# Two more PSUM banks for the first batch's transposes and head pairs, and the second batch's keys loaded ahead of w_in

## The chip, the cores and the metric

One core of one Trainium2 chip (trn2). The metric is the device time of the whole kernel in microseconds; runs of one kernel mostly agree within 0.3%.

## The reference

Grouped attention followed by a feed-forward layer with squared ReLU, cut to what matters:

```python
q: (8, 16, 384, 64)   k, v: (8, 4, 384, 64)      # batch, heads, tokens, head size
attn = softmax(q @ k.T / 8) @ v                   # four query heads share one key head
x = attn as (3072, 1024)
out = max(x @ w_in, 0)**2 @ w_out                 # w_in (1024, 2048), w_out (2048, 1024)
```

## The kernel before

Work goes batch by batch. Scores of a batch go to PSUM banks 0 to 3, ACT takes their exponentials, "head pairs" multiply these with the values, their outputs are transposed to x, and the feed-forward tiles of one batch are interleaved with the scores of the next. Of the eight PSUM banks, 6 and 7 are meant for the feed-forward layer.

The order in which TensorE's instructions stand is not written by hand. A Python program (the recorder) keeps a clock for each engine and an estimated end for each load, made of constants in the code, and at each step places the candidate that its estimates call ready, by rank: score bursts 0, first batch's transposes 1, head pairs 2, transposes of outputs 3, second batch's transposes 4.5, feed-forward pieces 5. Second, the chip then runs TensorE's instructions in that fixed order: a semaphore wait (the engine standing still until another engine or a load reports that it is done) that the estimates thought over holds all that stands behind it.

```python
def pick(allowed):                       # which PSUM bank
    i = min(allowed, key=lambda i: (max(R.when(writes=[("bank", i)]), R.clock["tensor"]), used[i]))
...
# GpSimd's own order at the start: loads (with a cast to bf16) and copies
load_q(0, 8, 12, 0.6); load_q(0, 12, 16, 0.6)
dup_k(0, 1, 2)
load_w_in(0)
dup_k(0, 2, 3)
load_k(1)                                # second batch's keys
dup_k(0, 3, 4); aug_v(0, "gpsimd")
load_q(1, 0, 8); load_q(1, 8, 16)
load_w_in(1); load_v(1)
dup_k(1)                                 # one copy of 1.47 us
for i in range(2, 6): load_w_in(i)
aug_v(1, "gpsimd")
for i in range(6, 8): load_w_in(i)
...
LOW, MID, HIGH = tuple(range(6)), (4, 5), (6, 7)
...                                      # in the loop that places TensorE's work:
first = bool(sc_q) and sc_q[0][0] == 0   # scores of the first batch still to place
spare = MID if first else tuple(i for i in LOW if i not in held)
...
if turn_q and (b == 0 or pairs < 6 or x_done[0] == 8) and ...:
    cand.append((max(R.when(reads=src), open_bank(spare)) + wait, 3.5 * b + 1, "turn"))
...
ready = [x for x in cand if x[0] <= now + (0.0 if split else 0.05)]
what = min(ready, key=lambda x: x[1]) if ready else min(cand)
```

The softmax here doesn't subtract the row's maximum and nothing guards it: scores larger than these inputs give would overflow.

Of the kernel before, what the change touches and what calls it, by code (L numbers as in the profile page):

```python
# [141 lines left out]
def bass_gqa_attention__then__ffn_squared_relu_kernel(  # L142
# [64 lines left out]
    def load_k(b, after=()):  # L207
        st = b % NST
        R.add("gpsimd", lambda g: g.dma_start(  # L209
            k_st[st].ap().rearrange("p (g j) d -> p g (j d)", j=NJ),  # L210
            k[b].rearrange("g (p j) d -> p g (j d)", j=NJ)),
            reads=after, writes=[("k_st", st)], dma=f"k{st}", cost=1.1, issue=0.8)
# [19 lines left out]
    def load_v(b):  # L232
        st = b % NST
        R.add("gpsimd", lambda g: g.dma_start(
            v_st[st].ap().rearrange("p (g j) d -> p g (j d)", g=HKV),
            v[b].rearrange("g (p j) d -> p g (j d)", j=NJ)),
            writes=[("v_st", st)], dma=f"v{st}", cost=1.1, issue=0.8)

    def load_q(b, h0, h1, spread=0.0):
        st = b % NST  # L240
        i = R.add("gpsimd", lambda g: g.dma_start(  # L241
            q_st[st][:, h0:h1, :],
            q[b, h0:h1].rearrange("h (p j) d -> p h (j d)", j=NJ)),
            writes=[("q_st", st, h // 4, h % 4 // 2) for h in range(h0, h1, 2)], dma=f"q{st}_{h0}",
            cost=0.265 * (h1 - h0), issue=0.8)
        R.ops[i]["end"] += spread
# [4 lines left out]
    def load_w_in(i):  # L251
        R.add("gpsimd", lambda g: g.dma_start(
            w_in_sb[:, :, i * WC:(i + 1) * WC],
            moe_w_in[:, i * WC:(i + 1) * WC].rearrange("(c p) f -> p c f", p=128)),
            writes=[("w_in", i)], dma=f"wi{i}", cost=2.65, issue=0.9)
# [9 lines left out]
    def dup_k(b, g0=0, g1=HKV):  # L265
        n = (g1 - g0) * NJ
        src = (k_st[b % NST] if b else k_f32)[:, g0 * NJ:g1 * NJ, :].unsqueeze(2).to_broadcast([128, n, 2, D])
        dst = k_dup[b % 2][:, g0 * NJ:g1 * NJ, :, :]
        eng = "scalar" if b > 1 and not stretch[0] else "gpsimd"
        R.add(eng, lambda e: e.copy(dst, src) if eng == "scalar" else e.tensor_copy(dst, src),  # L270
              reads=[("k_st", b % NST) if b else ("k_f32", g) for g in range(g0, g1)],
              writes=[("k_dup", b % 2, g, x) for g in range(g0, g1) for x in range(2)], cost=0.125 * n)

    def aug_v(b, eng):
        R.add(eng, lambda e: e.tensor_copy(v_aug[b % 2][:, :, 0:D], v_st[b % NST][:, :, :]),  # L275
              reads=[("v_st", b % NST)], writes=[("v_aug", b % 2)], cost=0.4 if eng == "vector" else 0.85)
# [166 lines left out]
    held = set()  # L443
# [117 lines left out]
    load_q(0, 8, 12, 0.6)  # L561
    load_q(0, 12, 16, 0.6)
    dup_k(0, 1, 2)
    load_w_in(0)
    dup_k(0, 2, 3)
    load_k(1)
    dup_k(0, 3, 4)
    aug_v(0, "gpsimd")
    load_q(1, 0, 8)
    load_q(1, 8, 16)  # L570
    load_w_in(1)
    load_v(1)
    dup_k(1)
    for i in range(2, 6):
        load_w_in(i)
    aug_v(1, "gpsimd")
# [33 lines left out]
    LOW, MID, HIGH = tuple(range(6)), (4, 5), (6, 7)  # L610
# [63 lines left out]
    while av_q or av_open or sc_q or o_q or lanes or ff["now"] or ff["tiles"] or ff["down"]:  # L674
        now = R.clock["tensor"]
        first = bool(sc_q) and sc_q[0][0] == 0
        spare = MID if first else tuple(i for i in LOW if i not in held)
        if loaded + 1 < B and turned >= loaded and not turn_q:
            loaded += 1
            if loaded == 2:  # L680
# [163 lines left out]
```

## Time and profile before

| | before |
|---|---|
| median of 6 runs (lowest to highest) | 419.69 us (419.38 to 420.42) |
| span of the profiled run | 418.2 us |
| TensorE busy | 413.4 us, 99% |
| the first batch's twenty exponentials on ACT | 5.79 to 22.60 us, no pause |
| first row-split feed-forward tile (start of the interleaved part) | 28.75 us |
| wait for w_in block 3 there | 0.37 us |

Read it so: TensorE is busy for 99% of the span; in the first 23 us it follows ACT. The lines are in the prediction.

### The profile page before, as it was taken

Reading aid. Unit: us, or ns where it says so; the run is one execution under the profiler, and the core shown is the slowest. Engines: PE = TensorE matmul, PEld = TensorE weight load, DVE = VectorE, ACT = ScalarE, POOL = GpSimd, SP = SyncE. Lnnn points to the kernel's source line nnn. Section 1 sums busy time; section 2 is a strip of 40 time slices with the busy share of each in tenths; the row PEclk is TensorE's granted clock in tenths of the full one; section 3 lists DMA queues with packets and bytes.
Section 4 is the critical chain, followed back from the end, with each engine's and each line's share of the span. In section 5 each row is a group of like instructions: output and inputs, shape, how many; then the busy total and the mean of one; then the engine's idle time right before and its main releaser. Section 6 shows DMA issues by size and latency. Waiting matters only on the chain.

```text
span 418.2 us, 9601 instructions
## 1 busy us (share of the span) xinstructions
PE 413.4 (99%) x4308; PEld 236.2 (56%) x4331; DVE 198.6 (47%) x434; ACT 159.0 (38%) x181; POOL 48.0 (11%) x63
## 2 busy tenths in 40 slices
PE   9999999999999999999999999999999999999997
PEld 6666754557446574455645565456744557445544
DVE  3664751357413782156811666125841458324312
ACT  6948610495009610284104840069000870004300
POOL 8680000323030000200020000000000000000000
PEclk9999999999999999999999999999999999999999
DMA  9999999999996019900499005710052001420012
GB/s 179 190 190 200 206 188 170 260 190 120 187 186 101 2 39 201 209 7 2 61 211 183 2 2 107 183 52 2 3 125 77 27 2 20 122 79 10 0 74 78
DMA packets 96921, 44.40 MB, mean 106 GB/s; under 512 B 77296, under 2 KB 90864, under 8 KB 96880
## 3 DMA queue, kind: packets, MB, share of 16 engines
q0 software_dynamic: 36544, 17.44, 32.5%
q1 hardware_dynamic: 59664, 25.86, 27.7%
q8 instruction: 34, 0.56, 0.5%
q10 hardware_dynamic: 672, 0.49, 0.4%
q14 instruction: 7, 0.06, 0.0%
HBM read 35.65 MB, written 12.58 MB: 115 GB/s over the span
## 4 chain that ended last, share of the span: by engine, by line
PE 97%; ACT 2%; issue 0%; DVE 0%
PE ps L524 39%; PE ps L462 34%; PE ps L367 8%; PE ps L341 7%; PE ps L425 6%; ACT expT L351 2%; PE ps L588 1%; PE ps L400 0%; PE ps L298 0%; PE ps L315 0%; DVE y_sb L533 0%
## 5 line engine op out<-in xcount | busy, mean ns | idle before, releaser
L351 ACT ACTIVATE expT<-ps 128x1024 bf16<-128x1024 f32 (+1 forms) x146 | 136.0, 1022 | 133.4 <-PE ps L341 133.4
L524 PE MATMUL ps<-w_out_sb,h2T 128*128 128x512 bf16 (+2 forms) x761 | 165.7, 375 | 1.2
L462 PE MATMUL ps<-xT,w_in_sb 64*128 64x384 bf16 x1728 | 160.3, 323 | 0.0
L524 PEld LDWEIGHTS ps<-w_out_sb,h2T 128*128 128x128 bf16 x784 | 75.2, 98 | 86.6
L462 PEld LDWEIGHTS ps<-xT,w_in_sb 64*128 64x128 bf16 x1728 | 83.1, 94 | 57.8 <-DVE hr L475 2.1
L475 DVE TENSOR_SCALAR hr<-ps 128x384 f32<-128x384 f32 x108 | 55.2, 553 | 79.0 <-PE ps L462 79.0
L533 DVE COPY y_sb<-ps 128x512 f32<-128x512 f32 (+2 forms) x49 | 33.4, 681 | 112.3 <-PE ps L524 112.3
L341 PE MATMUL ps<-qT,kT 64*128 64x512 bf16 (+2 forms) x384 | 54.3, 326 | 0.3 <-ACT expT L351 0.3
L482 DVE TENSOR_TENSOR h2T<-hr 128x384 bf16<-128x384 f32 x102 | 50.0, 551 | 0.0
L367 PEld LDWEIGHTS ps<-v_aug,expT 128*128 128x128 bf16 x1152 | 37.0, 97 | 5.7 <-issue 1.1
L367 PE MATMUL ps<-v_aug,expT 128*128 128x65 bf16 x1152 | 39.1, 193 | 0.2 <-issue 0.2
L382 DVE TENSOR_TENSOR o_sb<-ps,rinv 128x384 bf16<-128x384 f32 x64 | 35.7, 558 | 2.2
L425 PE MATMUL ps<-xT,w_in_sb 128*128 128x384 bf16 x160 | 27.7, 326 | 0.0
L435 ACT ACTIVATE h2T<-hr 128x384 bf16<-128x384 f32 x20 | 10.3, 522 | 44.3 <-DVE hr L433 44.3
L341 PEld LDWEIGHTS ps<-qT,kT 64*128 64x128 bf16 x384 | 17.8, 94 | 15.6 <-issue 2.1
L275 POOL COPY v_aug<-v_st 128x768 bf16<-128x768 bf16 x8 | 6.6, 830 | 158.4 <-PE ps L367 99.5
L479 ACT ACTIVATE h2T<-hr 128x384 bf16<-128x384 f32 x6 | 3.1, 523 | 51.7 <-DVE hr L475 51.7
L425 PEld LDWEIGHTS ps<-xT,w_in_sb 128*128 128x128 bf16 x160 | 15.4, 98 | 9.7 <-DVE xT L406 0.2
L433 DVE TENSOR_SCALAR hr<-ps 128x384 f32<-128x384 f32 x20 | 11.0, 557 | 12.1 <-PE ps L425 12.1
L241 POOL DMA_DIRECT2D q_st<-in_q_dram x17 | 14.8, 883 | 0.9 <-POOLq L829 0.8
L376 DVE RECIPROCAL rinv<-ps 128x6 f32<-128x6 f32 x64 | 11.9, 186 | 4.4 <-PE ps L367 4.4
L209 POOL DMA_DIRECT2D k_st<-in_k_dram x7 | 5.3, 755 | 43.6 <-DMA qT<-q_st 43.6
(29 smaller groups left out, 65.2 us busy)
## 6 DMA issues: line engine op xcount, KB each, us to landing
out_dram<-y_sb SPq DMA_DIRECT2D x47, 256.0 KB, 2.6
q_st<-in_q_dram POOLq DMA_DIRECT2D x14, 384.0 KB, 8.2
w_in_sb<-in_moe_w_in_dram POOLq DMA_DIRECT2D x8, 512.0 KB, 14.8
w_out_sb<-in_moe_w_out_dram POOLq DMA_DIRECT2D x4, 1024.0 KB, 27.4
v_st<-in_v_dram POOLq DMA_DIRECT2D x8, 192.0 KB, 9.7
k_st<-in_k_dram POOLq DMA_DIRECT2D x7, 192.0 KB, 4.5
q_st<-in_q_dram POOLq DMA_DIRECT2D x3, 192.0 KB, 5.5
xT<-o_sb SPq DMA_TRANSPOSE x28, 2.8
```

What stands on the lines that cost most here:

```text
L241: i = R.add("gpsimd", lambda g: g.dma_start(q_st[st][:, h0:h1, :], q[b, h0:h1].rearrange("h (p j) d -> p h (j d)", j=NJ)), writes=[("q_st" ...
L341: mm = pe.matmul(ps[:, base + x, m * wide:(m + 1) * wide], kT[b % 2][64 * x:64 * x + 64, u, :], q_cols(b, u // NJ, x, c0, c0 + wide))
L351: R.add("scalar", lambda e: e.activation(dst, src, AF.Exp, scale=0.125), reads=keys, writes=[("expT", (b * NU + u) % NEX, t) for u, _, _ i ...
L367: m = pe.matmul(po[:, f - 6 * s2, 0:D + 1], w, v_aug[b % 2][:, g * NJ + j, 0:D + 1], start=(j == 0), stop=(j == NJ - 1))
L376: R.add("vector", lambda e: e.reciprocal(rinv[r].ap().unsqueeze(2), po[:, :, D:D + 1]), reads=[("bank", i)], writes=[("rinv", r)], cost=0.22)
L382: R.add("vector", lambda e: e.tensor_tensor(dst, srcv, rbv, ALU.mult), reads=[("bank", i), ("rinv", r)], writes=[("o_sb", o, s2)], cost=0.48)
L425: m = pe.matmul(bank(i)[:, 0:S], w_in_sb[:, kc, c * 128:(c + 1) * 128], xT[b % NXT][:, kc, :], start=(kc == 0), stop=(kc == NKC - 1))
L462: m = pe.matmul(bank(4 + xs[x])[:, 0:S], w_in_sb[r, kc, c * 128:(c + 1) * 128], xT[b % NXT][r, kc, :], start=(phase < 2 and kc == 0), stop ...
L475: R.add("vector", lambda e, r=r, i=i: e.tensor_scalar_max(hr[r][:, :], bank(4 + i)[:, 0:S], 0.0), reads=[("bank", 4 + i)], writes=[("hr", ...
L482: hr_read[r] = (R.add("vector", lambda e, c=c, r=r: e.tensor_tensor(h2T[:, c, :], hr[r][:, :], hr[r][:, :], ALU.mult), reads=[("hr", r)], ...
L524: m = pe.matmul(bank(i)[:, 0:n], h2T[:, c, i3 * 128:(i3 + 1) * 128], w_out_sb[:, c, c0:c1], start=(c == 0), stop=(c == NFC - 1))
L533: R.add("vector", lambda e: e.tensor_copy(ysl, bank(i)[:, 0:n]), reads=[("bank", i)], writes=[("y", yb)], cost=0.08 + n / 960)
```

## The change

Its intent: TensorE has room while ACT takes the first batch's exponentials. With banks 6 and 7 lent out while free, transposes and head pairs need not wait for banks 4 and 5; with the second batch's keys early, some of that batch's transposes fit in as well.

```diff
     dup_k(0, 1, 2)
+    load_k(1)
+    dup_k(0, 2, 3)
     load_w_in(0)
-    dup_k(0, 2, 3)
-    load_k(1)
     dup_k(0, 3, 4)
     aug_v(0, "gpsimd")
     load_q(1, 0, 8)
+    dup_k(1, 0, 2)
     load_q(1, 8, 16)
+    dup_k(1, 2, 4)
     load_w_in(1)
     load_v(1)
-    dup_k(1)
...
-        spare = MID if first else tuple(i for i in LOW if i not in held)
+        spare = tuple(i for i in MID + HIGH if i not in held) if first else tuple(i for i in LOW if i not in held)
```

## The prediction

> **What bounds the kernel now.** I read the page of the profile first, for the engines as a whole, then the same measure in stretches of time, then the timeline of single engines at the start, where the change acts.
>
> From the page (busy us, share of the span, instructions):
>
> ```profile
> PE 413.4 (99%) x4308; PEld 236.2 (56%) x4331; DVE 198.6 (47%) x434; ACT 159.0 (38%) x181; POOL 48.0 (11%) x63
> PE 97%; ACT 2%; issue 0%; DVE 0%
> ```
>
> The second line is the chain that ended last: TensorE carries 97% of it. The span can therefore shrink only where TensorE waits or does filler. ACT is on the chain for about 2% (8 us), and that is the start. The timeline of ACT there (start, duration, group):
>
> ```profile
> 5.79 16.81 ACT L351 ACTIVATE expT<-ps 128x768 bf16<-128x768 f32 x20 [0.76 <-PE ps L341]
> ```
>
> All twenty exponentials of the first batch run from 5.79 to 22.60 us. They are merged in one row whose length is the whole stretch, so ACT does not pause once. This stretch is set by ACT, and TensorE only follows. The stretches of time of all engines, and of single lines (L425: first feed-forward tiles; L298 and L315: transposes of keys and queries), first row 5.79 to 22.60, second 22.60 to 28.75:
>
> ```profile
> 5.79:22.60 16.81, 2.22 (x9) 0.79 (x9) 1.00 1.51 190
> 22.60:28.75 6.15, 4.40 (x24) 2.10 (x23) 1.00 1.36 184
> ...
> 22.60:28.75 6.15, 1.16 (x12) 0.80 (x12) 1.00 1.36 184
> ...
> 22.60:28.75 6.15, 1.00 (x12) 0.75 (x12) 1.00 1.36 184
> ```
>
> Columns after the length of the stretch: TensorE busy with the count of matmuls in brackets, weight loads likewise, granted clock, DMA share, GB/s. Rows one and two are L425: of its 32 to 33 early feed-forward matmuls only 9 fit into the ACT-bound stretch, 24 come after it. Rows three and four: the second batch's 12 key and 12 query transposes all come after it, where TensorE has no time to spare. These 24 transposes are what the change can bring forward.
>
> What comes directly after is the timeline of weight loads where the second batch's scores and the row-split feed-forward tiles begin:
>
> ```profile
> 28.75 0.44 PEld L462 LDWEIGHTS ps<-xT,w_in_sb 64*128 64x128 bf16 x8 [0.32 <-DVE hr L433]
> 29.47 0.11 PEld L341 LDWEIGHTS ps<-qT,kT 64*128 64x128 bf16 x4 [0.28 <-DVE hr L433]
> 29.70 0.64 PEld L462 LDWEIGHTS ps<-xT,w_in_sb 64*128 64x128 bf16 x8
> 30.71 0.44 PEld L462 LDWEIGHTS ps<-xT,w_in_sb 64*128 64x128 bf16 x8 [0.37 <-DMA w_in_sb<-in_moe_w_in_dram]
> ```
>
> The last row decides my prediction. At 30.34 us TensorE already waits 0.37 us for a block of w_in to land. It is the fourth block (index 3, for tiles 6 and 7): issued at 15.98, 14.8 us to landing by the table of DMA issues, so 30.75. The list of waits has this one wait for w_in in the whole kernel.
>
> GpSimd's timeline, which issues these loads:
>
> ```profile
> 5.78 0.90 POOL L252 DMA_DIRECT2D w_in_sb<-in_moe_w_in_dram  x1
> 6.67 0.52 POOL L270 CAST k_dup<-k_f 128x384 bf16<-128x384 f32 x1
> 7.12 0.76 POOL L209 DMA_DIRECT2D k_st<-in_k_dram  x1
> ...
> 13.68 1.47 POOL L270 COPY k_dup<-k_st 128x1536 bf16<-128x1536 bf16 x1 [1.20 <-DMA k_st<-in_k_dram]
> 15.09 3.52 POOL L252 DMA_DIRECT2D w_in_sb<-in_moe_w_in_dram  x4
> ```
>
> Landings, issue plus latency from the same table: w_in block 0 at 12.6, the second batch's keys 13.6, its first half of queries 16.8, second half 18.9, w_in block 1 21.4, values 22.5, w_in blocks 2 and 3 at 26.7 and 30.75. Latencies grow while the rate in 1-us stretches stays at 167 to 212 GB/s from 5 us on: the queue never runs dry, so an arrival is set by the bytes ahead of it.
>
> **What the Trainium skill says.** "TensorE: Matmul & The Clock Gate", section Back-to-back issue gap: an isolated matmul takes N/2.4 ns plus about 2.5 ns, 56 ns for 128 columns. The trace agrees: the 24 transposes start at 24.50 and the next matmul's weights at 25.84, 1.34/24 = 56 ns each, so I use this and not the 219 ns of the records, which hold latency. "PSUM — Partial Sum Buffer", section Engine vs sequencer instructions: matmuls start and complete in program order. So one matmul ordered ahead of its data holds all behind it; the row at 30.71 is such a wait. The same page, PSUM bank collisions raise a hardware error: a bank has to be guarded until its reader is done. No run shows a collision, but the trace shows how long a bank is held: a head pair from 14.24 (first matmul) to 15.79 (end of the VectorE multiply), 1.55 us; a transpose of its output from 15.22 to 16.06, 0.84 us. "DMA: Bandwidth & Descriptors", section Issuing engines are not separate DMA queues: all DMAs run on the same 16 engines and interleave. The trace agrees: while the query transpose that SyncE issued at 18.86 is in flight (11.5 us, to 30.4), w_in blocks 2 and 3 land 4.2 and 4.0 us after what was ahead; the next blocks need 2.1 to 2.8.
>
> **The change part by part.**
> First, banks. During the first batch's scores, head pairs and transposes could use only banks 4 and 5; now also 6 and 7 while no feed-forward tile holds them. A round of 1.90 us (14.24 to 16.14) uses 1.55 + 0.84 = 2.39 of 2 x 1.90 = 3.80 bank-us, so the two banks were 63% full. More banks remove some waits of TensorE of 0.2 to 0.4 us, but ACT does not pause, so the stretch keeps its 16.81 us. The gain inside it is nil; only work moved into it counts. And the first feed-forward tiles take banks 6 and 7 from 15.34 us on and keep them until all eight chunks of x are there, so the freedom lasts only until then.
>
> Second, the keys. Ahead of w_in block 0 they skip 512 KB, at 190 GB/s 2.76 us, and land at 10.85 instead of 13.6. The duplication is cut in two, 1.47/2 = 0.74 us each. Its first half ends at about 11.6, against 15.15. In return w_in block 0 lands 192 KB = 1.03 us later, at 13.6; its first reader is the matmul at 15.34, so nothing waits.
>
> Third, what moves. The order is fixed: keys of head group 0, queries of 0, keys of 1, queries of 1, keys of 2 and 3. The first (3 x 56 = 0.17 us) can now run between 11.6 and 15. The second needs queries that still land at 16.8 (the same bytes ahead of them), when banks 6 and 7 are held again and head pairs go first; and the program stops such transposes after six pairs (about 19.7). I expect 0.17 us certain and up to 0.17 + 0.34 + 0.17 = 0.67 us with luck; all 24 would be 1.34.
>
> Fourth, where it ends. TensorE reaches the wait for w_in block 3 0.17 to 0.67 us earlier, at 29.7 to 30.2. Bytes ahead of that block are the same, the query transpose starts when the same bytes have landed, so it lands at 30.75 again: the wait grows from 0.37 to 0.54 to 1.04 us. The only work that can slip in front is the third score burst (four matmuls of 256 columns, two at a time: 2 x 0.107 = 0.21 us), if the first exponential of this batch (29.90 to 30.87) ends before 30.7, which needs 0.2 us or more. Sum: 0 to 0.2 us gained, plus perhaps 0.1 for nicer order; later blocks land at least 1 us before their use. 419.73 - 0.3 = 419.4.
>
> **The rivals.** (a) All 24 transposes move and w_in block 3 does not hold: 419.73 - 1.34 = 418.4. For it: TensorE has room in the ACT-bound stretch, since 23 feed-forward matmuls are left for later for lack of x, not of time. Against it: queries at 16.8, and the row at 30.71. (b) A transpose is ordered before its queries have landed, as the program places instructions by its own fixed estimates, and TensorE stands still up to a microsecond around 16 us; then ACT gets its first pause. ACT has one score burst (0.9 us of work) in hand, so 0 to 0.7 us is lost, of which the 0.37 us of slack at w_in hides a part: 419.7 to 420.1. Against it: the transposes have low rank in the order. (c) Splitting the copy holds GpSimd up: free at 9.98 after the first query load, it waits for the keys to 10.85, copies to 11.6, issues the second query load (0.88), copies again (0.74) and issues w_in block 1 at 13.2 for 10.84, then values and w_in block 2 at about 14.9 for 15.09. Block 1 lay 10.6 us in the queue before, so 2.4 us less of that is hidden: no change, 419.7.
>
> **Range and chances.** Mechanisms reach from -1.3 to +0.4 us, and the three runs of before spread over 1.04 us. A range of 418.7 to 420.1 holds the likely part. 2% would be 8.4 us, over six times the largest of them: within 2% is all but sure.
>
> **What would show it.** Right: ACT's row of twenty exponentials still some 16.8 us long without a pause; the keys' copy on GpSimd in two of about 0.74 us, the first from about 10.9; three key transposes of the second batch before 15 us and most of the others after 22; the wait for w_in longer than 0.37 us and ending near 30.7; from there on the same timeline. Wrong: an ACT pause between 6 and 22 us, the w_in wait gone or ending over 0.5 us elsewhere, or a changed course after 50 us.

## More of the kernel before

A short form of TensorE's order from 5 to 16 us, which no profile row shows at a glance, in letters: S a score piece of two matmuls, Q and K transposes of queries and keys, A a head pair, O a transpose of its output, F a feed-forward matmul, w filler; the digits count matmuls.

```
before: S4 Q3 K3 w2 S2 Q6 S2 K3 w1 S2 w3 S2 Q6 S2 K3 S2 Q6 A9 S4 A18 S2 A9 S2 O3 S4 A18 S2 O3 F2 S2
```

## The result, and the profile after

The changed kernel takes 420.96 us (median of 6 runs, 420.44 to 422.62) against 419.69. The ratio is 1.0036, 95% interval 1.0017 to 1.0054. Ratios here and below are the mean time of one kernel's fast runs over that of the other's fast runs of the same rounds, so not quite the ratio of the medians quoted. It is the same within 2%, and slower by 1.3 us, outside the range predicted.

A warning on the two traces: the profiled run of the changed kernel took 420.44 us, the fastest of its six; that of before took 420.3, one of its slowest. Laid side by side they differ by 0.3 us of span only. So I compare what the stages do, not the ends. The start of the exponentials is a draw, too: 5.37 to 5.89 us in the twenty profiles.

ACT in the first stretch, after (start, duration, group, idle time before it and what ended it); the row to set beside it is the single one from 5.79 in the prediction:

```profile
5.37 1.51 ACT L351 ACTIVATE expT<-ps 128x768 bf16<-128x768 f32 x2 [0.42 <-PE ps L341]
7.67 2.21 ACT L351 ACTIVATE expT<-ps 128x768 bf16<-128x768 f32 x3 [0.79 <-PE ps L341]
10.23 7.29 ACT L351 ACTIVATE expT<-ps 128x768 bf16<-128x768 f32 x8 [0.35 <-PE ps L341]
17.83 6.16 ACT L351 ACTIVATE expT<-ps 128x1024 bf16<-128x1024 f32 x7 [0.32 <-PE ps L341]
```

The twenty exponentials now stand in four pieces (2 + 3 + 8 + 7). Three pauses, 0.79 + 0.35 + 0.32 = 1.46 us, each ended by a score burst of TensorE. They end at 17.83 + 6.16 = 23.99 us, 1.39 later than before, although they began 0.42 earlier: the stretch is 18.62 us long, not 16.81. Of these 1.81 us, 1.46 are the pauses. The other 0.35 come with them: exponentials that follow each other without a pause overlap in the trace of before (by 0.03 to 0.24 us), and a pause takes one such overlap away. What TensorE did ahead of each pause, from its timeline of weight loads, after:

```profile
6.16 0.17 PEld L298 LDWEIGHTS ps<-ident,k_dup 128*128 128x128 bf16 x3 [0.57 <-POOL k_dup L270]
6.85 0.34 PEld L315 LDWEIGHTS ps<-ident,q_st 128*128 128x128 bf16 x6 [0.52 <-DMA q_st<-in_q_dram]
7.29 0.10 PEld L341 LDWEIGHTS ps<-qT,kT 64*128 64x128 bf16 x2
...
9.47 0.33 PEld L367 LDWEIGHTS ps<-v_aug,expT 128*128 128x128 bf16 x9 [0.50 <-POOL v_aug L275]
9.85 0.10 PEld L341 LDWEIGHTS ps<-qT,kT 64*128 64x128 bf16 x2
...
13.62 0.21 PEld L298 LDWEIGHTS ps<-ident,k_dup 128*128 128x128 bf16 x3
...
16.78 0.35 PEld L315 LDWEIGHTS ps<-ident,q_st 128*128 128x128 bf16 x6 [0.85 <-DVE o_sb L382]
17.09 0.10 PEld L425 LDWEIGHTS ps<-xT,w_in_sb 128*128 128x128 bf16 x1
17.40 0.10 PEld L341 LDWEIGHTS ps<-qT,kT 64*128 64x128 bf16 x2 [0.21 <-issue]
```

Each pause has a wait of TensorE ahead of it. At 6.16 three key transposes have waited 0.57 us for GpSimd's copy, which in this run waited for its load. At 6.85 six query transposes have waited 0.52 us for their load, and the third score burst stands behind them, at 7.29; before, that burst stood ahead of them (rows below). At 9.47 the first head pair has waited 0.50 us for GpSimd's copy of the values, with a burst behind it. At 16.78 six query transposes of the second batch have waited 0.85 us. The row names VectorE as what ended that wait; but the load they read was issued at 9.35 and needed 7.3 us by the table of issues, so it landed at 16.65: the load came last. The row at 13.62 is the one early key transpose that the change was made for, and the first feed-forward matmuls stand at 14.39, 0.95 us earlier than before. The two rows of before to set beside 6.85 and 7.29, burst first and the transposes after it:

```profile
6.89 0.10 PEld L341 LDWEIGHTS ps<-qT,kT 64*128 64x128 bf16 x2
7.16 0.34 PEld L315 LDWEIGHTS ps<-ident,q_st 128*128 128x128 bf16 x6 [0.17 <-issue]
```

The order after, in letters:

```
after:  S4 Q3 K3 Q6 S2 K3 S2 w3 S2 w3 A9 S2 Q6 S2 K3 S2 Q6 A9 S4 A18 S2 O3 K3 S2 O3 F2 S4 A18 S2 Q6 F1 S2
```

GpSimd's side, after:

```profile
6.05 0.75 POOL L209 DMA_DIRECT2D k_st<-in_k_dram  x1
7.25 0.90 POOL L252 DMA_DIRECT2D w_in_sb<-in_moe_w_in_dram  x1
...
11.00 0.83 POOL L270 COPY k_dup<-k_st 128x768 bf16<-128x768 bf16 x1 [0.77 <-DMA k_st<-in_k_dram]
...
12.63 0.83 POOL L270 COPY k_dup<-k_st 128x768 bf16<-128x768 bf16 x1
```

The keys, issued at 6.05, land at 10.9 (4.9 us by the table of issues) and are copied in two parts of 0.83 us. The first w_in block lands at 7.25 + 7.0 = 14.2 us, against 12.6 before; block 3 at 30.9 against 30.7.

Where the second batch begins, after:

```profile
29.92 1.94 PEld L462 LDWEIGHTS ps<-xT,w_in_sb 64*128 64x128 bf16 x24
```

There is no wait for block 3 any more, because TensorE comes later than it landed. A yardstick for the whole: the time T at which the long row of head-pair weight loads of the second batch starts (108 in every profile), near 50 us. It is 48.58 before and 49.29 after. In the twenty profiled runs (before, after and e1 to e18), time minus T lies between 371.15 and 372.06 us, while T itself spreads over 5.0 us. So the large differences arise before 50 us; one of less than 0.9 us can't be placed in this way. Before and after themselves have 371.72 and 371.15.

### The profile page after: what moved, and what is told of

Read it like the earlier page. It is cut to its first block, busy times and chain, and to the rows that moved or that the text cites. A ratio compares the mean times of both kernels' runs of the same rounds, so it can differ in the third digit from the quotient of the medians.

```text
span 418.5 us, 9601 instructions
## 1 busy us (share of the span) xinstructions
PE 412.3 (99%) x4308; PEld 235.4 (56%) x4331; DVE 199.1 (48%) x434; ACT 159.2 (38%) x181; POOL 48.0 (11%) x64
## 3 DMA queue, kind: packets, MB, share of 16 engines
q0 software_dynamic: 36544, 17.44, 32.7%
## 4 chain that ended last, share of the span: by engine, by line
PE 97%; DMA 1%; POOL 1%; issue 0%; DVE 0%; ACTq 0%
PE ps L524 39%; PE ps L462 34%; PE ps L367 9%; PE ps L341 8%; PE ps L425 6%; DMA k_f<-in_k_dram 1%; PE ps L400 0%; PE ps L315 0%; POOL k_dup L270 0%; PE ps L298 0%; POOL w_in_sb L252 0%; POOL v_aug L275 0%; POOL k_st L209 0%; DVE o_sb L382 0%; ACTq L223 0%
## 5 line engine op out<-in xcount | busy, mean ns | idle before, releaser
L425 PE MATMUL ps<-xT,w_in_sb 128*128 128x384 bf16 x160 | 27.9, 326 | 0.0
L341 PEld LDWEIGHTS ps<-qT,kT 64*128 64x128 bf16 x384 | 17.8, 94 | 15.3 <-issue 2.9
L425 PEld LDWEIGHTS ps<-xT,w_in_sb 128*128 128x128 bf16 x160 | 15.4, 98 | 9.9 <-DVE hr L433 0.3
L241 POOL DMA_DIRECT2D q_st<-in_q_dram x17 | 14.8, 886 | 0.9 <-POOLq L830 0.8
```

The costliest lines, as they stand in the source:

```text
L241: i = R.add("gpsimd", lambda g: g.dma_start(q_st[st][:, h0:h1, :], q[b, h0:h1].rearrange("h (p j) d -> p h (j d)", j=NJ)), writes=[("q_st" ...
L341: mm = pe.matmul(ps[:, base + x, m * wide:(m + 1) * wide], kT[b % 2][64 * x:64 * x + 64, u, :], q_cols(b, u // NJ, x, c0, c0 + wide))
L425: m = pe.matmul(bank(i)[:, 0:S], w_in_sb[:, kc, c * 128:(c + 1) * 128], xT[b % NXT][:, kc, :], start=(kc == 0), stop=(kc == NKC - 1))
```

## The experiments

All were timed in five rounds against the kernel before, whose 55 runs in these five sets took 419.25 to 421.64 us, with medians of 419.45 to 419.70 in a set. All gave correct results. "Order" always means the order of TensorE's instructions. The edits are to the changed kernel unless another base is named.

| run | what | ratio to before (95%) | median us | T in its profile (time of that run) |
|---|---|---|---|---|
| e1 | the change again | 1.0035 (1.0023 to 1.0048) | 421.37 | 49.14 (420.37) |
| e2 | banks part alone | 1.0033 (1.0015 to 1.0050) | 420.90 | 49.47 (421.34) |
| e3 | keys part alone | 1.0014 (0.9999 to 1.0030) | 420.23 | 50.41 (421.76) |
| e4 | change, second batch's queries late | 1.0037 (1.0025 to 1.0049) | 421.16 | 49.41 (421.16) |
| e5 | change, third score burst first | 1.0035 (1.0020 to 1.0050) | 421.10 | 49.46 (420.64) |
| e6 | e5, and first head pair later | 1.0056 (1.0023 to 1.0089) | 421.26 | 51.42 (422.78) |
| e7 | e6, and second batch's queries late | 1.0036 (1.0023 to 1.0049) | 421.08 | 49.04 (420.60) |
| e8 | keys part, values after w_in block 3 | 1.0015 (0.9999 to 1.0031) | 420.13 | 48.19 (419.46) |
| e9 | change with true estimates | 1.0034 (1.0022 to 1.0046) | 421.19 | 49.47 (421.19) |
| e10 | banks part with true estimates | 1.0007 (0.9995 to 1.0019) | 419.99 | 48.49 (420.15) |
| e11 | keys part, feed-forward later | 1.0033 (1.0021 to 1.0045) | 421.25 | 48.67 (420.58) |
| e12 | before, w_in block 0 late | 1.0065 (1.0045 to 1.0085) | 422.69 | 53.20 (424.69) |
| e13 | keys part, copy at its old place | 1.0018 (1.0001 to 1.0035) | 420.33 | 50.67 (421.84) |
| e14 | before, copy between the loads | 1.0087 (1.0067 to 1.0107) | 423.78 | 51.63 (423.56) |
| e15 | e10, values after w_in block 3 | 1.0020 (1.0008 to 1.0032) | 420.47 | 49.16 (420.91) |
| e16 | before, values after w_in block 3 | 1.0004 (0.9992 to 1.0016) | 419.81 | 48.26 (419.70) |
| e17 | e9, values after w_in block 3 | 1.0025 (1.0005 to 1.0046) | 420.40 | 48.73 (420.12) |
| e18 | banks part, one estimate true | 1.0028 (1.0012 to 1.0045) | 420.93 | 49.13 (421.19) |

### First set: which part, and which of the waits

**e1**, no edit.

> The changed kernel once more, unaltered, as the yardstick of this set. Order theory (the freed banks let TensorE's program put transposes and a head pair in front of score bursts before their data is there, and ACT runs dry): ratio to before 1.002 to 1.005, and the row of twenty exponentials again broken by pauses of ACT, 1.0 to 1.8 us in sum between 5 and 25 us. Load theory (the new order of loads and the split copy on GpSimd cost the time): the same ratio. Chance theory (the first measurement was a bad draw of transfer times): ratio within 1.001.

The loss is real: 1.0035. Two of the three pauses are back in other sizes (0.72 and 0.51 us); the middle one is absent, since here the first head pair waited only 0.16 us for the values.

**e2**, base the kernel before:

```diff
-        spare = MID if first else tuple(i for i in LOW if i not in held)
+        spare = tuple(i for i in MID + HIGH if i not in held) if first else tuple(i for i in LOW if i not in held)
```

> Only the banks part of the change; loads and copies on GpSimd as in the kernel before. Order theory: the pause before the third exponential (0.8 us in the changed kernel) and the one at the first head pair (0.35) are here, the one at 17.5 us (0.3) is not, since the second batch's keys come late and no query transpose is drawn forward; ratio 1.001 to 1.004. Load theory: as before, within 1.001, no pause of ACT.

ACT, banks part alone:

```profile
5.46 1.51 ACT L351 ACTIVATE expT<-ps 128x768 bf16<-128x768 f32 x2 [0.49 <-PE ps L341]
7.92 2.21 ACT L351 ACTIVATE expT<-ps 128x768 bf16<-128x768 f32 x3 [0.95 <-PE ps L341]
10.48 13.33 ACT L351 ACTIVATE expT<-ps 128x768 bf16<-128x768 f32 x15 [0.35 <-PE ps L341]
```

Two pauses, 0.95 and 0.35 us, and none at 17.5: as the order theory said. The ratio, 1.0033, is that of the whole change. I also built, and did not run, the kernel before with banks 6 and 7 open to nothing but that one group of six query transposes: TensorE's order came out the same as in e2. One decision at 7 us carries the whole new order.

**e3**, the load and copy part of the diff on the kernel before. TensorE's order is unaltered.

> Only the load and copy part; banks 4 and 5 alone for the first batch as in the kernel before. TensorE's instructions then stand in exactly the order of the kernel before. Order theory: within 1.001 of before, ACT without a pause over 0.2 us. Load theory: slower by most of the 1.3 us, 1.002 to 1.004.

ACT runs without a pause (16.92 us in one row). The ratio, 1.0014, sits between the two theories, with an interval that just holds 1. Its six runs take 419.51 to 421.76: most are like before, some are slow. The profile caught the slowest one:

```profile
32.53 0.44 PEld L462 LDWEIGHTS ps<-xT,w_in_sb 64*128 64x128 bf16 x8 [2.43 <-DMA w_in_sb<-in_moe_w_in_dram]
```

Here w_in block 3 landed at 32.5 us and TensorE stood 2.43 us for it.

**e4**:

```diff
-        if turn_q and (b == 0 or pairs < 6 or x_done[0] == 8) and ...
+        if turn_q and (b == 0 or (pairs < 6 and w == "k") or x_done[0] == 8) and ...
```

> The changed kernel, but the second batch's query transposes may not be drawn forward into the first batch's scores (its key transposes still may). Order theory: the 0.85 us wait of TensorE at 16.8 us and the ACT pause after it are gone, the pauses near 7 and 10 us stay; 0.0 to 0.4 us faster than the changed kernel of the same set (the pause of 0.3 us less, but 0.34 us of transposes back after the scores). If the 16.8 us wait were the main cost: 0.8 us or more faster than the changed kernel. Load theory: equal to the changed kernel.

The wait at 16.8 us and its pause are gone, and the time is that of the changed kernel (1.0037 to 1.0035), at the small end of what was expected. The pause of 0.3 us and the 0.34 us of transposes moved back may cancel; that is argued. In this profile the first feed-forward matmul also stood 0.58 us for w_in block 0 (landed at 14.8), and ACT paused 0.20 us after it: the first sight of a wait that the next set brings out.

### Second set: take the waits out one by one

**e5**, **e6**, **e7**. The six transposes of the first batch may be placed only after the third score piece; in e6 the first head pair only after the sixth; in e7 also the edit of e4.

```diff
+            ... and ((b, g, w) != (0, 1, "q") or sc_q[0] > (0, 2))           # e5, e6, e7: turn
-            if needs <= scored and ff["b"] >= ...
+            if (b or c or sc_q[0] > (0, 5)) and needs <= scored and ...     # e6, e7: head pair
```

> The changed kernel, but the second query transposes of the first batch (six of them, head group 1) may not stand ahead of the third score burst. Order theory: ACT's pause before the third exponential (0.7 to 0.95 us in the runs so far) is gone. The first head pair then stands even earlier, in front of two score bursts, and waits for GpSimd's copy of the values, so that pause stays or grows to 0.3 to 1.0 us, and the one near 17.5 us stays. 0 to 0.7 us faster than the changed kernel, still slower than before. If these two waits were harmless: equal to the kernel before.

> The same, and the first head pair may not stand ahead of the sixth score piece either. Order theory: no pause of ACT before 14 us; the wait of TensorE at 16.8 us for the second batch's queries stays, with an ACT pause of 0.2 to 0.5 us near 17.5. About 1.0 us faster than the changed kernel, within 0.4 us of before. Rival (the cost lies after the scores, in the second batch's course or the loads): equal to the changed kernel.

> All three waits taken out by order: as the run above, and the second batch's query transposes only after the scores. Order theory: ACT runs its twenty exponentials without a pause over 0.2 us; time within 0.3 us of before or up to 0.3 us faster, 1.0 to 1.5 us faster than the changed kernel; a wait for the block of w_in of up to 2.4 us may show as in the kernel with the keys alone. Rival: equal to the changed kernel.

In e5 the first pause shrank to 0.32 us, and the head pair, now earlier still, waited 0.95 us for the values and made a pause of 0.79: one wait took the other's place, and the time stayed (1.0035). The second batch's queries were waited for 1.08 us here, with a pause of 0.55. In e6 and e7 I had expected about the time of before; both missed. TensorE's weight loads in e6:

```profile
15.76 0.13 PEld L425 LDWEIGHTS ps<-xT,w_in_sb 128*128 128x128 bf16 x2 [1.75 <-issue]
16.20 0.11 PEld L341 LDWEIGHTS ps<-qT,kT 64*128 64x128 bf16 x4 [0.32 <-issue]
```

There was a fourth wait, which my theory did not have. The first feed-forward matmul, with a score burst behind it, stood 1.75 us at 15.76 us. The row says "issue", which is what the profile says where it sees no releaser, but w_in block 0 was issued at 6.97 and needed 8.7 us, so it landed at 15.7. ACT then paused 1.37 us; it had also paused 0.51 us at 7.77, where none was expected (see e17 for that one). In e7 the same matmul waited 0.69 us; block 0 landed at 14.4. Both parts of the change feed this wait: the keys ahead of block 0 make it late, and with head pairs and output transposes earlier its first reader comes earlier.

**e8**, base e3: the values' load behind w_in blocks 2 and 3, and their copy behind block 7's load.

> The keys part alone, and the second batch's values loaded after w_in blocks 2 and 3 instead of ahead of them (192 KB, about 1 us), so block 3 lands about 1 us earlier; TensorE's order stays that of the kernel before. If the 0.14% of the keys part alone comes from waiting for block 3 (2.4 us in its profiled run): back to within 0.05% of before or faster, no wait for w_in over 1.4 us. If it comes from anything earlier: 1.001 to 1.002 again.

Block 3 landed at 29.1 us, no wait for it is seen, and the ratio, 1.0015, is that of e3. So nothing here says that block 3 alone is what the keys part costs, though the interval (0.9999 to 1.0031) excludes neither case. And this profile is of the fastest of six runs (419.46; the slowest took 422.00), so it shows the good case.

### Third set: tell the program the truth

**e9**, and **e10** on the banks part alone (with 1.5 us for block 0): the recorder's estimates are moved to about what the traces show. A bank with a head pair half written is now also called held, so that no feed-forward tile can take it, a hazard that lending 6 and 7 out brings in by the code.

```diff
-    load_q(0, 4, 8)                     # first batch's second query load
+    load_q(0, 4, 8, 0.6)
     load_w_in(0)
+    R.ops[-1]["end"] += 2.2
-    load_q(1, 0, 8)
+    load_q(1, 0, 8, 1.7)
-    ... cost=0.4 if eng == "vector" else 0.85)                              # copy of the values
+    ... cost=0.4 if eng == "vector" else 0.85 if b else 1.35)
```

> The changed kernel, whole, but the program that orders TensorE's instructions is told landings near those measured: first batch's second query load 0.6 us later, values' copy 0.5, w_in block 0 2.2, second batch's first query load 1.7 (and a bank with an open head pair counts as held). Loads stand in the same order as in the changed kernel. Theory now (TensorE stands in front of data that has not landed, at four places, with score bursts behind it; the fourth is the first feed-forward matmul, which waits for w_in block 0): no wait of TensorE for such data over 0.4 us before 25 us, ACT without a pause over 0.3 us, ratio 0.999 to 1.001. Rival (something else in the changed order costs it, as the run with three waits out suggests): 1.003 again.

> The banks part alone (loads as before), with such estimates. Theory now: the loss of the banks part alone (1.0033) is gone, 0.999 to 1.001; w_in block 0 lands by 14 us. Rival: 1.003.

ACT in e10:

```profile
7.31 15.32 ACT L351 ACTIVATE expT<-ps 128x768 bf16<-128x768 f32 x18 [0.31 <-PE ps L341]
```

One pause of 0.31 us, and a ratio of 1.0007 with five runs inside 0.42 us, in place of 1.0033 and 2.2 us: no longer placing TensorE's work ahead of late data repairs the banks part, as expected. (e18 below has the held bank too and is slow, so that edit is not the repair.) With the keys part in (e9) ACT is as clean, one pause of 0.20 us, but the ratio is 1.0034, against my expectation. So the pauses are not the whole account of the full change: with them gone the time is lost elsewhere. Where the second batch begins in e9:

```profile
31.57 0.47 PEld L462 LDWEIGHTS ps<-xT,w_in_sb 64*128 64x128 bf16 x8 [0.99 <-issue]
```

It waited 0.99 us for w_in block 3, which landed at 31.4 us in this run (again under "issue"). And with feed-forward matmuls put off, 19 instead of 17 of them stand behind the last transposes, 2 x 0.163 = 0.33 us.

**e11**, base e3: `R.ops[-1]["end"] += 3.5` after the load of w_in block 0.

> The keys part alone (1.0014), but the program believes w_in block 0 3.5 us later, so that the first two feed-forward matmuls stand one round later, about 19 instead of 15.4 us; TensorE's order before them is that of the kernel before. If the keys part costs time because w_in block 0 at times lands after 15.4 us and TensorE stands before it: 0.9995 to 1.0005 and all six runs within 1 us. Otherwise 1.001 to 1.002 and single runs 1 to 2 us slow.

A miss: 1.0033. ACT is clean (16.87 us in one row), and T is 48.67 where 48.2 is the value of a run without waits (e8, e16); 0.33 of this 0.47 is again two feed-forward matmuls more after the scores. But that profile is of its fastest run, and what made the other four up to 1 us slower was not seen.

**e12**, base the kernel before: the instruction that loads w_in block 0 is moved behind the second batch's first query load when the program is written out, after the order has been fixed.

> The kernel before, with one thing done: w_in block 0 is issued after the second batch's first query load (576 KB more ahead of it), the order of TensorE unaltered. Theory now: it lands near 16 us instead of 12.6, TensorE stands 0.5 to 1.5 us before the first feed-forward matmul at 15.4, ACT pauses 0.3 to 1.2 us near 16 to 17 us, ratio 1.001 to 1.003. If such a wait were hidden by the room in the first stretch: within 1.0005 and no pause.

This is the wait by itself, with TensorE's order exactly that of before. Block 0 landed at 17.5, later than I had worked out, TensorE stood 2.61 us, ACT paused 2.79, and the ratio is 1.0065, above the 1.001 to 1.003 expected. The room of TensorE in the first stretch does not hide it.

```profile
17.53 0.13 PEld L429 LDWEIGHTS ps<-xT,w_in_sb 128*128 128x128 bf16 x2 [2.61 <-DMA w_in_sb<-in_moe_w_in_dram]
18.93 1.02 ACT L355 ACTIVATE expT<-ps 128x1024 bf16<-128x1024 f32 x1 [2.79 <-PE ps L345]
```

(Lines stand four lower in this kernel.py: L429 is L425 elsewhere.) This profile, of the slowest of its six runs, shows one thing more, in TensorE's stretches of time (busy, matmuls, granted clock, DMA share, GB/s):

```profile
15.00:17.00 2.00, 0.09 (x2) 1.00 1.54 193
17.00:19.00 2.00, 1.47 (x8) 0.54 1.52 195
19.00:21.00 2.00, 2.00 (x26) 0.50 1.49 195
21.00:23.00 2.00, 2.00 (x21) 0.50 1.49 196
23.00:25.00 2.00, 2.00 (x33) 0.75 1.38 189
```

After the standstill the granted clock (the share of its full clock that TensorE gets) is half for 6.8 us: the rows lose 0.92 + 2 x 1.00 + 0.50 = 3.42 us of full clock, twice that in time. The Trainium skill, "TensorE: Matmul & The Clock Gate", section What's actually happening, says that idle time of about 3.4 us closes the clock gate to half. This run agrees with the half, not with the length: it stood 2.61 us. e6, after its 1.75 us, shows it too (0.50 between 17 and 19 us). A wait of this kind can therefore cost more than its length: T is 4.9 us later here than in e16. A mean clock under 1.000 goes with it: half clock for 6.8 of 420 us makes 0.992, for 3.4 us 0.996. It is 0.992 or 0.996 in four of the six runs of e12, in two of e6, and in the slowest run of the changed kernel (422.62 us), of e2 (422.72), e5 (422.77), e8 (422.00), e9 (421.67), e14 (424.54) and e17 (421.72); in all 55 runs of before it is 1.000.

### Fourth and last set: what the keys part costs, and what is left

**e13**, base e3, the copy of the keys undivided and after the loads; **e14**, base the kernel before, the copy divided and between the loads.

> The second batch's keys loaded ahead of w_in block 0 as in the changed kernel, but GpSimd's copy of them whole and at its old place, after the loads; banks as before, TensorE's order as before. If holding GpSimd up is what the keys part costs: 0.9995 to 1.0007. If the order of bytes is: 1.001 to 1.002 as with the whole keys part.

> Loads in the order of the kernel before, but the copy split and put between the loads as in the changed kernel; as the keys land at 13.6 us here, GpSimd is held up from about 10 to 14 us, 3 us longer than in the changed kernel. If the hold-up costs: 1.002 to 1.005, fewer GB/s between 12 and 18 us, w_in block 3 later than 31 us. If the order of bytes costs: within 1.001.

e13 costs the same as the whole keys part (1.0018), which speaks for the order of bytes and against the copies between the loads as its cost. It does not exclude them: its interval, 1.0001 to 1.0035, reaches into the 0.9995 to 1.0007 expected for the other case. Its profile, of its slowest run, shows both waits for w_in, block 0 at 15.6 and block 3 at 32.7:

```profile
15.61 0.11 PEld L425 LDWEIGHTS ps<-xT,w_in_sb 128*128 128x128 bf16 x2 [0.48 <-DMA w_in_sb<-in_moe_w_in_dram]
```

```profile
32.80 0.44 PEld L462 LDWEIGHTS ps<-xT,w_in_sb 64*128 64x128 bf16 x8 [2.26 <-DMA w_in_sb<-in_moe_w_in_dram]
```

e14 shows that holding GpSimd up is not harmless if it lasts: it waited 3.65 us for the keys, the DMA engines fell to 70 and 91 GB/s in the 4 us after 14 us (193 and 195 before), block 3 landed at 33.9, and the ratio is 1.0087, above the 1.002 to 1.005 expected. ACT shows no pause (16.74 us in one row); the loss seen is after it, where TensorE stood 1.70 us at 25.2 for w_in block 1. In the changed kernel GpSimd's wait is 0.77 us.

In the twelve profiles with the keys first, w_in block 0 landed at 13.5 to 15.7 us, 14.5 in the middle. In the seven with block 0 first in its old place it landed at 12.5 to 14.0, 13.1 in the middle. Its first reader stands at 15.3 us in the order of before. Early keys thus put the block's landing into the reader's reach in the slower draws, and block 3 tends to be later too, though the ranges overlap (30.1 to 32.7 us, 31.3 in the middle, in ten keys-first profiles with the values in their old place; 30.5 to 31.3, 30.6 in the middle, in four with block 0 first, e14 left out).

**e15**, **e16**, and of the last set **e17**: the values' load behind block 3, on e10, on the kernel before and on e9.

> The banks part with true estimates (1.0007), and the second batch's values loaded after w_in block 3. That kernel waited 0.40 us for block 3; it lands about 1 us earlier now, so no wait for it: 0.9990 to 1.0003. If block 3 does not set the time there: 1.0007 again.

> The kernel before with only the values loaded after w_in block 3, TensorE's order unaltered. No wait for block 3 (0.37 us in the profile of before): 0.9990 to 1.0000, and the slower runs of before (420.4 and above) gone. If waits for block 3 are rare: 1.000.

> The whole change with true estimates (1.0034), and the second batch's values loaded after w_in block 3, so that the block lands about 1 us earlier. If the wait for block 3 is what is left: no wait for it over 0.3 us, 1.000 to 1.0015. If not: 1.003 again.

e15 and e17 missed their numbers. e16 (1.0004) falls to its second theory: the wait for block 3 is rare in the kernel before and worth nothing in its median. e15 is slower than e10; in its profiled run a query load landed 1 us later than elsewhere (10.9 us) and TensorE stood 0.76 us for it. That tells of a transfer that varied in this one run; whether the others are slow for the values' later load or by such draws is not shown. As e10 and e15 have the same order of TensorE, and e15's interval (1.0008 to 1.0032) lies above 1, e10's level time holds for its own order of loads only. e17 has TensorE's order of e9 and shows no wait for block 3, as expected. Its median is 0.8 us under e9's (of another set), but 1.0025 is not before's time; the interval, wide also since one run of before in that set took 421.64, holds both 1.0015 and e9's 1.0034. So the wait for block 3 may be part of what was left in e9; it is not shown to be. And ACT is not clean in e17's profile:

```profile
7.83 15.32 ACT L351 ACTIVATE expT<-ps 128x768 bf16<-128x768 f32 x18 [0.57 <-PE ps L341]
...
7.23 0.11 PEld L590 LDWEIGHTS ps<-const-bfloat16-1.0 128*128 128x128 bf16 x2 [0.71 <-DVE kT L304]
```

Ahead of this pause TensorE's filler stood 0.71 us, not for a load but for VectorE's copy of a transposed key (kT). By the code the filler writes bank 7, and by the recorder the key transpose just before it now sits in bank 7, which the kernel before never lends; so the filler waits until VectorE has read it, with the third score burst behind. This is a fifth wait that the lent banks bring, and it isn't one for late data. It stands in eight of the profiles (e5 to e7, e9, e10, e15, e17, e18), 0.62 to 0.72 us long, each with a pause of ACT of 0.20 to 0.57 us near 7.5 us. In the changed kernel itself the six query transposes stand in that place.

**e18**, base e2: only `load_q(0, 4, 8, 0.6)`, and the held bank.

> The banks part alone, with only the first batch's second query load believed 0.6 us later. The six query transposes then stand behind two score bursts, but the first head pair moves ahead of two others, before its values are copied. If the head pair's wait costs as much as the transposes': ACT pauses 0.5 to 1.0 us near 9.5 us, ratio 1.001 to 1.0035. If only the transposes' wait mattered: 1.0007 or less, as with all estimates true.

The transposes stand behind two score bursts, and the first head pair is now what waits:

```profile
9.16 0.33 PEld L367 LDWEIGHTS ps<-v_aug,expT 128*128 128x128 bf16 x9 [0.97 <-POOL v_aug L275]
```

ACT pauses 0.81 us for it, and the ratio is 1.0028: this wait alone costs about as much as the two together did.

No version beat the kernel before; e16 and e10 come level with it within their intervals, e3 and e8 just so (both from 0.9999).

## Why the prediction was wrong

The step that failed is the first part of the sum: "ACT does not pause, so the stretch keeps its 16.81 us. The gain inside it is nil; only work moved into it counts." I had shown that ACT sets the stretch, and took from it that more freedom for TensorE could not lengthen it. But the profile of before shows only that this order fed ACT in time. With two banks for everything, a transpose or a head pair became placeable only when a bank came free, which was mostly later than its data; the scarcity held back what the estimates would have placed too early. The recorder says so itself: printed while it builds the kernel before, the six query transposes have their data at 6.26 us and a bank at 6.68, by its own estimates, and the first head pair 8.71 and 10.56; in e2 the banks are free at 4.67 and at once. With four banks the estimates decide, they are 0.5 to 2.2 us too early (the corrections of e9), and TensorE stands in order before the data with score bursts behind it. In place of nil the term measured 1.81 us (a stretch of 18.62 us for 16.81), or 1.39 by the end of the exponentials (22.60 to 23.99), which had begun 0.42 earlier. e2 shows it in the banks part alone, e10 shows it gone with truer estimates, e5 and e18 show one such wait taking another's place.

Point by point, by its own steps:

- "One matmul ordered ahead of its data holds all behind it": right, and I applied it only to the wait at 30.34 us. Rival (b) described the mechanism for the second batch's queries and set it aside since "the transposes have low rank". That holds for the second batch's; the first batch's have rank 1 and the head pairs 2, and these made the two larger pauses. Even the low-ranked one came, at 16.78.
- The second term, the keys: landing 10.85 predicted, 10.9 measured; first copy done at 11.6 predicted, 11.83 measured. Block 0 "at 13.6; its first reader is the matmul at 15.34, so nothing waits": it landed at 14.2 in both profiles of the changed kernel (13.5 to 15.7 in the twelve with the keys first), and the reader moved to 14.39. The prediction took the landing from the bytes ahead alone; the block was also issued 1.47 us later (7.25 for 5.78) and needed 7.0 us for 6.8. e12 shows what this wait costs when it is long. Rival (c), GpSimd's hold-up: right for its 0.77 us, and e14 shows where it stops being right.
- The third term, 0.17 to 0.67 us moved forward: 3 + 6 transposes moved, 9 x 56 ns = 0.50 us. Right in size; but the six queries came with the wait and the pause of 0.32 us that rival (b) feared. (The 56 ns per transpose are the trace's. The section that the prediction cites, Back-to-back issue gap in the Trainium skill's "TensorE: Matmul & The Clock Gate", gives this figure for an isolated matmul and about 81 ns for a stream of weight loads and matmuls, which is what stands in this trace; the trace decides.)
- The fourth, block 3 at 30.75: it landed at 30.9. (In the profile of before it landed at 30.66, after 14.7 us; the 14.8 us are the median of all eight blocks.) The wait was to grow to 0.54 to 1.04 us; it vanished, since TensorE came later. In e9, where ACT is nearly clean, it is there with 0.99.
- The sum for the profiled runs: 1.39 by which the exponentials end later, less 0.50 moved forward, less the 0.37 no longer waited = 0.52 us; T moved by 0.71. The medians moved by 1.27, since that profile of before is of a slow run and that of after of the fastest.

Shown: that the banks part alone costs 1.0033 and that four waits in front of late data exist, each with its pause of ACT, and a fifth of the filler for bank 7; that truer estimates repair the banks part with its own order of loads; that w_in block 0 late, with TensorE's order unaltered, costs. Not shown: that the pauses are the whole loss of the full change, since e9 has hardly any and keeps 1.0034. Shown in single profiles, not in medians: that the slow runs of the keys part are runs in which blocks 0 and 3 land late. Open: why the time that block 0 needs varies from 6.6 to 8.7 us in the twelve profiles with the keys first, and what remains in e7, e9, e11 and e17, whose profiles of one run each do not account for their medians.

## What to carry to other kernels

A scarce buffer can be the brake that keeps an in-order engine from running into its own late inputs; before lending it more, check for every reader that becomes placeable whether its data has landed by then in the trace, not by the scheduler's estimate, and which other instructions use that buffer (here the filler). An engine that "has room" still must not stand still while others hang on what stands behind the wait; ask what is next in its order, not how full it is. And profile a run whose time is near the median before reading small differences.

## What the Trainium skill lacked or had wrong

- "TensorE: Matmul & The Clock Gate", section Why this matters for your kernels, asks for no gaps of TensorE over about 3 us. Here standstills of 2.61 us (e12) and 1.75 us (e6) were followed by a granted clock of 0.50 for 6.8 and 3.4 us; waits of 2.43 us (e3) and 2.26 us (e13) were not, with a mean clock of 1.000. The gap's length alone does not decide.
- No page says how far the landing of one and the same transfer varies from run to run: w_in block 3, in one order of loads, landed between 30.1 and 32.7 us in ten profiles.
- No page says that a wait shown as "issue" or under another engine can be a DMA: it was in the waits of 1.75 us (e6), 0.99 us (e9) and 0.85 us (the changed kernel), by the landing in the table of issues.
